# All scores of a pair of heads in one stretch: causal attention with three score buffers, ahead of a routed expert layer

## The chip, the cores and the metric

One core of one Trainium2 chip. The metric is the device time of one execution in microseconds (us), median of several; all values are fp32.

## The reference, cut to what matters

```python
# q, k, v: (8 batches, 8 heads, 576, 64), s: (8, 8, 576)
scores = q @ k.T / sqrt(64)                       # causal
cum = cumsum(maximum(s, 0), axis=-1)
bias = -(cum[:, :, :, None] - cum[:, :, None, :])
attn = exp(scores + minimum(bias, 0) - max)       # masked above the diagonal
attn = attn / (attn.sum(-1) + 1e-9)
x = (attn @ v) -> (8, 576, 512)
# then a router picks one of 8 experts per token (with a "locality gate" that can
# keep the previous token's expert): out = p[e] * (relu(x @ w1[e]) @ w2[e]), 512 -> 1024 -> 512
```

A pair of heads goes through these steps: score products and exponentials, products with the values, row sums (for the division), a product that turns the result back to rows of tokens and carries the router's weights along (the "turn back"), and the divisions. The kernel works through 32 pairs of heads in some 300 us and then through the experts in some 560 us. The routing of finished batches (sorting tokens by expert) is slipped in between pairs of heads, from about the tenth pair on.

## The kernel before

TensorE writes its products into banks of PSUM; the other engines read them there. Of the eight banks that the kernel uses, two score buffers take four, and four single banks hold values (`o0`, `o1`) and the turned-back result (`b0`, `b1`). The scores of a pair come in four units, two at a time, with work of the pairs before in between:

```python
def sums(n):                  # row sums: one-column products with a column of ones
    ...
                    for p in (p, P - TL) if 2 * g + t == NF else (p,):
                        mm(xs["o", 1][p : p + TL, i : i + 1], lhsT=w, rhs=one, start=True, stop=True)
    nc.vector.reciprocal(recs[:, n], xs["o", 1][:, at : at + 2 * NB])
# ... cut
for n in range(NPAIR + 1):
    # ... loads cut
    if n < NPAIR:
        scores(n, 0)                              # products, ScalarE exponentials, GpSimd masks
        scores(n, 1)
    if n:
        values(n - 1, 0, (0, 1))
        values(n - 1, 1, (0, 1))
        add_up(n - 1)                             # VectorE additions, for the sums
        copy(n - 1, 0)                            # VectorE: values out of PSUM
    if n > 1:
        back(n - 2, 1)                            # rows(): turn back; divide(): VectorE divisions
    for f in plan.pop((n, 0), ()): f(bank)        # routing work
    if n < NPAIR:
        scores(n, 2)
        scores(n, 3)
    if n:
        values(n - 1, 1, (2, 3, NF))
        sums(n - 1)                               # ends in bank o1, like group 1 of the values
        copy(n - 1, 1)                            # reads o1: after the sums
        back(n - 1, 0)                            # into b0
    for f in plan.pop((n, 1), ()): f(bank)
```

Of the kernel before, what the change touches and what calls it, by code (L numbers as in the profile page):

```python
# [10 lines left out]
F32 = mybir.dt.float32  # L11
I32 = mybir.dt.int32
Act = mybir.ActivationFunctionType
Alu = mybir.AluOpType
# [32 lines left out]
GROUPS = ((0, 2 * P), (2 * P, S))  # L47
MIDS = (P, 13 * TL // 2)
# [3 lines left out]
    ((1, 0, P, 2 * P), (0, 0, 0, 2 * P), (NF, 1, TS, S)),  # L52
    ((0, 1, 2 * P, S), (3, 1, 3 * P, S)),
    ((1, 1, 2 * P, S),),
    ((2, 1, 2 * P, S),),
# [11 lines left out]
def kernel(  # L67
# [30 lines left out]
    with ExitStack() as main:  # L98
# [40 lines left out]
        tail = attention(tc, q, k, vm, s, w_gate, w_local, ident, lg, recs, const, new_x, plan)  # L139
        tables = sort.tables()  # L140
        check = in_range(main.enter_context(tc.tile_pool(name="g_sb", bufs=1)), nc, recs, sort.total, sort.ones, out_of)
        hooks = [(0, tail), (2, last.stages[0]), (6, last.stages[1]), (11, last.stages[2]),
# [49 lines left out]
def attention(ctx, tc, q, k, vm, s, w_gate, w_local, ident, lg, recs, keep, new_x, plan):  # L192
# [11 lines left out]

# [5 lines left out]
    def pool(name, bufs, **kw):  # L210
        return ctx.enter_context(tc.tile_pool(name=name, bufs=bufs, **kw))
# [5 lines left out]
    ps_s = pool("ps_s", 2, space=PSUM)  # L217
    ps_o = pool("ps_o", 1, space=PSUM)

# [46 lines left out]
    idle = ps_o.tile([P, 512], F32, name="idle", tag="b0")  # L266

    def spin(n):
        for i in range(n):
            mm(idle[:, :P], lhsT=ident, rhs=ident, start=True, stop=True)  # L270
# [9 lines left out]
    for g, (q0, q1) in enumerate(GROUPS):  # L280
        rel = t_in.tile([BH, q1], F32, name=f"rel{g}")
        nc.vector.tensor_scalar(rel, cum[:, :q1], cum[:, MIDS[g] : MIDS[g] + 1], None, Alu.subtract)
        for c, a in enumerate(KEYS):
            if a + P <= q1:
                tr(bps[:, at : at + BH], rel[:, a : a + P], ident[:BH, :BH])
                bias_of[c, g] = at
                at += BH
# [3 lines left out]
    nc.vector.memset(bias[: P - TL, at : at + BH], MASKED)  # L291
    tmp.close()
# [3 lines left out]
    def scores(n, u):  # L296

        b, hp = divmod(n, HP)
        qb, kb = ins[b]
        ps = ps_s.tile([P, 2, 512], F32, name="ps", tag="s")  # L300
        sc = scs[n, u] = p_sc.tile([P, 2, sum(z - a for _, _, a, z in UNITS[u])], F32, name=f"sc{u}")
        for c, g, a, z in UNITS[u]:
            at = PIECE[c, g][1]
            for h in range(2):
                d = slice(DH * h, DH * h + DH)
                mm(ps[:, h, at : at + z - a], lhsT=kb[d, hp, KEYS[c] : KEYS[c] + P], rhs=qb[d, hp, a:z],  # L306
                   start=True, stop=True)
        for c, g, a, z in UNITS[u]:
            at = PIECE[c, g][1]
            for h in range(2):  # L310
                i = bias_of[c, g] + 2 * n + h
                nc.scalar.activation(sc[:, h, at : at + z - a], ps[:, h, at : at + z - a], Act.Exp,  # L312
                                     bias=bias[:, i : i + 1], scale=scale)
        diag = [PIECE[c, g][1] for c, g, a, z in UNITS[u] if a == KEYS[c]]
        if diag:
            step = diag[1] - diag[0] if len(diag) > 1 else P
            x = sc[:, :, diag[0] : diag[0] + step * len(diag)].rearrange("p h (n c) -> p h n c", c=step)[:, :, :, :P]
            nc.gpsimd.affine_select(out=x, in_=x, compare_op=Alu.is_ge, fill=0.0, base=0,  # L318
                                    pattern=[[0, 2], [0, len(diag)], [1, P]], channel_multiplier=-1)
        if (NF, 1) in PIECE and PIECE[NF, 1][0] == u:  # L320
            at = PIECE[NF, 1][1]
            x = sc[:, :, at : at + TL]
            nc.gpsimd.affine_select(out=x, in_=x, compare_op=Alu.is_ge, fill=0.0, base=P - TL,
                                    pattern=[[0, 2], [1, TL]], channel_multiplier=-1)

    def piece(n, c, g, a=0):

        u, at, q0, q1 = PIECE[c, g]
        at += max(0, a - q0)
        return scs[n, u][:, :, at : at + q1 - max(a, q0)]  # L330

    def add_up(n):

        add = nc.vector.tensor_tensor
        low = xs["sum", 0] = p_sm.tile([P, 2, P], F32, name="sum0")
        add(low, piece(n, 0, 0, P), piece(n, 1, 0), op=Alu.add)
        high = xs["sum", 1] = p_sm.tile([P, 2, S - 2 * P], F32, name="sum1")
        add(high, piece(n, 0, 1), piece(n, 1, 1), op=Alu.add)
        for c in (2, 3, NF):
            x = high[:, :, PIECE[c, 1][2] - 2 * P :]  # L340
            add(x, x, piece(n, c, 1), op=Alu.add)  # L341

    def values(n, g, cs):

        b, hp = divmod(n, HP)
        q0, q1 = GROUPS[g]
        if cs[0] == 0:
            xs["o", g] = ps_o.tile([P, 512], F32, name=f"o{g}", tag=f"o{g}")
        o = xs["o", g]
        for c in cs:  # L350
            a, z = PIECE[c, g][2:]
            w = piece(n, c, g)
            for h in range(2):
                mm(o[DH * h : DH * h + DH, a - q0 : z - q0], lhsT=vas[b % 2][:, c, 2 * hp + h, :], rhs=w[:, h],  # L354
                   start=(c == 0), stop=(c == (1, NF)[g]))

    def copy(n, g):
        q0, q1 = GROUPS[g]
        x = xs["t", g] = (keep if g else p_sm).tile([P, q1 - q0], F32, name=f"xT{g}")
        nc.vector.tensor_copy(x, xs["o", g][:, : q1 - q0])  # L360

    def halves(g):

        q0, q1 = GROUPS[g]
        for a in range(0, q1 - q0, TL):
            yield a // P, a, a % P

    def sums(n):

        at = S - 2 * P  # L370
        for g in range(2):
            for h in range(2):
                for t, a, p in halves(g):
                    w = piece(n, 0, 0) if g + t == 0 else xs["sum", g]
                    w = w[:, h, (a if g + t == 0 or g else a - P) :][:, :TL]
                    i = at + 2 * (2 * g + t) + h
                    for p in (p, P - TL) if 2 * g + t == NF else (p,):
                        mm(xs["o", 1][p : p + TL, i : i + 1], lhsT=w, rhs=one, start=True, stop=True)  # L378
        nc.vector.reciprocal(recs[:, n], xs["o", 1][:, at : at + 2 * NB])

    def rows(n, g, ps):
        hp = n % HP
        w = turn[:, hp].rearrange("p h w -> p (h w)")
        for t, a, p in halves(g):
            mm(ps[p : p + TL, t * 2 * HW : (t + 1) * 2 * HW], lhsT=xs["t", g][:, a : a + TL], rhs=w,  # L385
               start=True, stop=True)

    def divide(n, g, ps):

        b, hp = divmod(n, HP)  # L390
        if (b, "x") not in xs:
            xs[b, "x"] = new_x(b)
        for t0, t1, m in (((0, 2, P),), ((2, 4, P), (4, 5, TL)))[g]:
            k, i = t1 - t0, t0 - 2 * g
            x = xs[b, "x"][:m, t0:t1, 2 * hp * HW : (2 * hp + 2) * HW].rearrange("p t (h w) -> p t h w", w=HW)
            y = ps[:m, 2 * i * HW : 2 * (i + k) * HW].rearrange("p (t h w) -> p t h w", h=2, w=HW)
            rec = recs[:m, n, 2 * t0 : 2 * t1].rearrange("p (t h) -> p t h", h=2)
            nc.vector.tensor_tensor(x, y, rec.unsqueeze(3).to_broadcast([m, k, 2, HW]), op=Alu.mult)

# [13 lines left out]
    def back(n, g, ps=None):  # L413
        ps = ps_o.tile([P, 512], F32, name=f"b{g}", tag=f"b{g}") if ps is None else ps
        rows(n, g, ps)
        divide(n, g, ps)
        if g and n % HP == HP - 1:
            logits(n // HP)

    for n in range(NPAIR + 1):  # L420
        b, hp = divmod(n, HP)
        if b + 1 < B:
            if hp == 0:
                new_batch(b + 1)
            load_qk(b + 1, slice(hp, hp + 1))
            if hp == 1:
                load_v(b + 1, slice(0, HP))
        if n < NPAIR:
            scores(n, 0)
            scores(n, 1)  # L430
        if n:
            values(n - 1, 0, (0, 1))
            values(n - 1, 1, (0, 1))
            add_up(n - 1)
            copy(n - 1, 0)
        else:
            spin(8)
        if n > 1:
            back(n - 2, 1)
        for f in plan.pop((n, 0), ()):  # L440
            f(bank)
        if n < NPAIR:
            scores(n, 2)
            scores(n, 3)
        if n:
            values(n - 1, 1, (2, 3, NF))
            sums(n - 1)
            copy(n - 1, 1)
            back(n - 1, 0)
        else:  # L450
            spin(8)
        for f in plan.pop((n, 1), ()):
            f(bank)
    assert not plan
    return lambda bank: back(NPAIR - 1, 1, bank(1)[0])
# [786 lines left out]
```

## Time and profile before

| | before |
|---|---|
| median of 3 runs | 866.54 us (865.88 to 870.08) |
| profiled run | span 865.4 us, mean granted TensorE clock 0.997 |
| period of one pair of heads, no routing work beside it | 8.63 us |
| first expert product starts at | 302.06 us |

The prediction below shows and reads the lines of the page of the profiled run and of its chain: the work that ended last, followed back step by step to what each piece waited for. The granted clock is the share of full speed that TensorE was allowed. "Period" is the time from one pair's first scores to the next pair's.

### The profile page before, as it was taken

The numbers are of one execution on the slowest core, as the hardware profiler recorded it, in microseconds if no ns is written. First come the engines' busy times: TensorE is split into PE (matmuls) and PEld (weight loads), VectorE is DVE, ScalarE is ACT, GpSimd is POOL, SyncE is SP. The second block draws the span as 40 slices with busy tenths as digits, with TensorE's granted clock in tenths as the row PEclk, the third lists the DMA queues.
The fourth block names the chain that finished last, engine by engine and source line by source line (L and its number), as shares of the span: only waits on it lengthen the run. The fifth ranks groups of instructions, "written<-read, shape, count | busy, mean of one in ns | idle before, by whom it ended". The sixth has DMA issues, their size and how long they took to land.

```text
span 865.4 us, 17612 instructions
## 1 busy us (share of the span) xinstructions
PE 847.9 (98%) x7051; PEld 594.0 (69%) x7051; DVE 314.1 (36%) x837; ACT 185.5 (21%) x493; POOL 188.5 (22%) x289
## 2 busy tenths in 40 slices
PE   9999999999999999999899999999999999999996
PEld 7777677776777786586577766677657755776662
DVE  3566776678787757301111111111111111111111
ACT  5565555545555300000000000000000000000000
POOL 4322327226454205201110011000111001100001
PEclk9999999999999999999999999999999999999999
DMA  9163155833542609996599766994689935996001
GB/s 312 38 200 122 51 172 179 313 119 143 181 148 84 230 6 300 409 394 206 206 340 394 279 204 222 348 394 175 235 300 373 380 132 202 320 400 254 21 13 39
DMA packets 61403, 191.24 MB, mean 221 GB/s; under 512 B 7965, under 2 KB 9277, under 8 KB 61312
## 3 DMA queue, kind: packets, MB, share of 16 engines
q1 hardware_dynamic: 52272, 159.27, 51.9%
q0 software_dynamic: 8896, 30.47, 9.4%
q8 instruction: 57, 0.93, 0.4%
q10 hardware_dynamic: 144, 0.29, 0.1%
q14 instruction: 34, 0.28, 0.1%
HBM read 166.76 MB, written 23.76 MB: 220 GB/s over the span
## 4 chain that ended last, share of the span: by engine, by line
PE 97%; DVE 1%; issue 1%; POOL 0%; POOLq 0%; DVEq 0%
PE yp L1150 30%; PE hp L1126 28%; PE ps L306 11%; PE o L354 11%; PE b L385 5%; PE o L378 4%; PE hp L1133 4%; PE xp L1101 2%; PE idle L270 1%; DVE r_u L925 0%; DVE r_v L926 0%; PE bank L921 0%; PE bank L936 0%; PE bank L954 0%; PE bank L955 0%
## 5 line engine op out<-in xcount | busy, mean ns | idle before, releaser
L1150 PE MATMUL yp<-w,hT 128*128 128x512 f32 (+1 forms) x528 | 221.1, 594 | 0.0
L1126 PE MATMUL hp<-xT,w 128*128 128x256 f32 (+1 forms) x1088 | 193.8, 339 | 1.9 <-DVE xT L1104 1.9
L1126 PEld LDWEIGHTS hp<-xT,w 128*128 128x128 f32 x1088 | 173.2, 192 | 26.4 <-issue 7.8
L312 ACT ACTIVATE sc<-ps,bias 128x320 f32<-128x320 f32 (+4 forms) x448 | 160.4, 466 | 117.2 <-issue 56.5
L1150 PEld LDWEIGHTS yp<-w,hT 128*128 128x128 f32 (+1 forms) x528 | 88.0, 180 | 100.5 <-issue 99.5
L1157 POOL DMA_INDIRECT out_dram<-y,at x38 | 38.4, 1012 | 457.6 <-DVE y L1156 442.7
L1141 ACT ACTIVATE hT<-hp 128x512 f32<-128x512 f32 x38 | 22.7, 597 | 509.5 <-PE hp L1126 425.6
L306 PE MATMUL ps<-qk 64*128 64x320 f32 (+4 forms) x896 | 109.0, 377 | 3.1 <-DVE r_v L926 2.8
L1139 DVE TENSOR_SCALAR hT<-hp 128x512 f32<-128x512 f32 x38 | 26.2, 690 | 220.4 <-PE hp L1126 187.7
L354 PE MATMUL o<-sc,va 128*64 128x320 f32 (+4 forms) x896 | 100.8, 364 | 0.0
L318 POOL TENSOR_SCALAR_AFFINE_SELECT sc<-sc 128x256 f32<-128x256 f32 (+1 forms) x96 | 59.2, 616 | 149.2 <-ACT sc L312 101.4
L306 PEld LDWEIGHTS ps<-qk 64*128 64x128 f32 x896 | 71.6, 186 | 25.6 <-issue 5.9
L354 PEld LDWEIGHTS o<-sc,va 128*64 128x64 f32 x896 | 56.8, 136 | 42.3 <-issue 18.6
L1156 DVE TENSOR_SCALAR y<-yp,gate 128x512 f32<-128x512 f32 x38 | 28.5, 751 | 134.8 <-PE yp L1150 134.8
L341 DVE TENSOR_TENSOR sum<-sum,sc 128x640 f32<-128x640 f32 (+2 forms) x96 | 61.6, 642 | 9.8 <-POOL sc L318 4.9
L1150 PE MATMUL yp<-x,hT 128*128 128x512 f32 (+1 forms) x144 | 64.8, 595 | 0.0
L1104 DVE COPY xT<-xp 128x512 f32<-128x512 f32 x38 | 26.2, 690 | 81.2 <-PE xp L1101 81.0
L385 PE MATMUL b<-turn,xT 128*64 128x146 f32 x566 | 50.5, 291 | 0.0
L1126 PE MATMUL hp<-xT,x 128*128 128x128 f32 (+1 forms) x320 | 50.1, 317 | 0.0
L1126 PEld LDWEIGHTS hp<-xT,x 128*128 128x128 f32 x320 | 46.1, 191 | 5.8 <-issue 2.6
L990 POOL DMA_INDIRECT x_rows<-x,r_slot_i x40 | 43.3, 1083 | 11.4 <-issue 8.5
L385 PEld LDWEIGHTS b<-turn,xT 128*64 128x64 f32 x566 | 38.6, 137 | 7.8
(156 smaller groups left out, 552.9 us busy)
## 6 DMA issues: line engine op xcount, KB each, us to landing
w<-in_w_dram SPq DMA_DIRECT2D x184, 512.0 KB, 8.4
x<-in_w_dram SPq DMA_DIRECT2D x56, 512.0 KB, 9.6
qk<-in_q_dram SPq DMA_DIRECT2D x32, 288.0 KB, 4.8
va<-in_vm_dram SPq DMA_DIRECT2D x35, 256.0 KB, 4.1
qk<-in_k_dram SPq DMA_DIRECT2D x31, 288.0 KB, 5.1
xg<-x_rows POOLq DMA_DIRECT2D x30, 293.0 KB, 8.6
x_rows<-r_empty SPq DMA_DIRECT2D x6, 293.0 KB, 4.2
xg<-x_rows SPq DMA_DIRECT2D x4, 293.0 KB, 5.2
```

What stands on the lines that cost most here:

```text
L306: mm(ps[:, h, at : at + z - a], lhsT=kb[d, hp, KEYS[c] : KEYS[c] + P], rhs=qb[d, hp, a:z], start=True, stop=True)
L312: nc.scalar.activation(sc[:, h, at : at + z - a], ps[:, h, at : at + z - a], Act.Exp, bias=bias[:, i : i + 1], scale=scale)
L318: nc.gpsimd.affine_select(out=x, in_=x, compare_op=Alu.is_ge, fill=0.0, base=0, pattern=[[0, 2], [0, len(diag)], [1, P]], channel_multipli ...
L341: add(x, x, piece(n, c, 1), op=Alu.add)
L354: mm(o[DH * h : DH * h + DH, a - q0 : z - q0], lhsT=vas[b % 2][:, c, 2 * hp + h, :], rhs=w[:, h], start=(c == 0), stop=(c == (1, NF)[g]))
L378: mm(xs["o", 1][p : p + TL, i : i + 1], lhsT=w, rhs=one, start=True, stop=True)
L385: mm(ps[p : p + TL, t * 2 * HW : (t + 1) * 2 * HW], lhsT=xs["t", g][:, a : a + TL], rhs=w, start=True, stop=True)
L990: self.s.nc.gpsimd.indirect_dma_start(out=next(self.s.views)[:, :], out_offset=bass.IndirectOffsetOnAxis(ap=self.slot[:z, m : m + 1], axis=0),
L1126: mm(y, lhsT=w[0][:, c, f : f + P], rhs=xT[i][:, c, :], start=(c == 0), stop=(c == DK - 1))
L1133: mm(y[d, m], lhsT=w[h ^ swap][:, c, f + h * HALF : f + h * HALF + HALF], rhs=xT[i][:, c, m], start=(c == 0), stop=(c == DK - 1))
L1150: mm(ps[n * m : n * m + m, :], lhsT=hT[i][:, c, a : a + m], rhs=wn[:, c, :], start=(c == 0), stop=(c == FK - 1))
L1157: nc.gpsimd.indirect_dma_start(out=next(outs)[:, :], out_offset=bass.IndirectOffsetOnAxis(ap=at[i, k][:, 0:1], axis=0), in_=y[:, :], eleme ...
```

## The change

The intent is to change TensorE's shape of product less often: all scores of a pair in one stretch, all other products of the pair before it in the next, so one passage each way per pair instead of two. Three double score buffers take six of the eight banks. The other two serve everything else, shared by column: values (0 to 320 and 0 to 256), turned-back tiles (0 to 438 and 0 to 292), sums (438 to 448 of bank 1) and a small 64-column score unit (448 to 512 of both). Queries are grouped as 320 and 256 instead of 256 and 320. The core of the diff:

```diff
+    banks = [ps_o.tile([P, 512], F32, name=f"o{g}", tag=f"o{g}") for g in range(2)]
+    SUMS, LAST = 3 * 2 * HW, 512 - TL
# ... cut: units, bias columns, masks, additions regrouped
@@ def values(n, g)
+        ...  products into banks[g] ...
+        x = xs["t", g] = p_sm.tile([P, q1 - q0], F32, name=f"xT{g}")
+        nc.vector.tensor_copy(x, banks[g][:, : q1 - q0])
@@ def sums(n)
-                        mm(xs["o", 1][p : p + TL, i : i + 1], lhsT=w, rhs=one, start=True, stop=True)
+                        mm(banks[1][p : p + TL, i : i + 1], lhsT=w, rhs=one, start=True, stop=True)
@@ rows() and divide() become one
+    def back(n):
+        for t0, t1, m in ((0, 3, P), (3, NF, P), (NF, NB, TL)):
+            k, ps = t1 - t0, banks[t0 >= 3]
+            ...
+            for t in range(t0, t1):
+                for a, g, at, p in halves(t):
+                    mm(ps[p : p + TL, t - t0], lhsT=xs["t", g][:, at : at + TL], rhs=w, start=True, stop=True)
+            ...
+            nc.vector.tensor_tensor(x, y, rec.unsqueeze(3).to_broadcast([m, k, 2, HW]), op=Alu.mult)
@@ the loop over pairs
+        if n:
+            add_up(n - 1)
         if n < NPAIR:
-            scores(n, 0)
-            scores(n, 1)
# ... cut: the rest of the old order
+            for u in range(len(UNITS)):
+                scores(n, u)
         for f in plan.pop((n, 0), ()):
             f(bank)
         if n:
-            values(n - 1, 1, (2, 3, NF))
+            values(n - 1, 0)
+            values(n - 1, 1)
             sums(n - 1)
-            copy(n - 1, 1)
-            back(n - 1, 0)
+            back(n - 1)
# ... cut
-    return lambda bank: back(NPAIR - 1, 1, bank(1)[0])
```

## The prediction

No term of its sum is among them: -11.0 + 22.4 + 22.3 - 4 - 0.5 came to +29 us on 866.5, so 896 us, and stands whole. The lost 0.09 to 0.10 us and the exposed loads are read from the passages at 125.81 and 126.94 shown: the record of the first pass of the new shape is 533 ns for the 429 of the later ones into scores, and 483 for 432 out of them. The fence with L938 and L939 stands as the test of whether waits go by bank, which waits A and B then assume. That an fp32 product is two passes is read from the counts: 384 passes of 320 columns at L306, for 32 pairs, two heads and three pieces.

> **What bounds the kernel now.** I read the page first (busy shares, slices, the chain that ended last), then the chain in order of time over one pair of heads, then TensorE's timeline in very narrow windows, then the groups by form.
>
> ```profile
> PE 847.9 (98%) x7051; PEld 594.0 (69%) x7051; DVE 314.1 (36%) x837; ACT 185.5 (21%) x493; POOL 188.5 (22%) x289
> ...
> PEclk9999999999999999999999999999999999999999
> ...
> PE yp L1150 30%; PE hp L1126 28%; PE ps L306 11%; PE o L354 11%; PE b L385 5%; PE o L378 4%; PE hp L1133 4%; PE xp L1101 2%; PE idle L270 1%; DVE r_u L925 0%; DVE r_v L926 0%; PE bank L921 0%; PE bank L936 0%; PE bank L954 0%; PE bank L955 0%
> ```
>
> TensorE is busy 98% of the span, so time moves only by (a) how long its own stream takes and (b) new holes in it. The change touches attention alone: the first 300 us, 32 pairs. One pair in the chain, in order of time (start, length, what):
>
> ```profile
> 123.48 1.88 PE o L354 x16
> 125.36 0.74 PE b L385 x10
> 126.10 1.28 PE ps L306 x8
> 127.38 1.13 PE o L354 x12
> 128.50 1.12 PE o L378 x39
> 129.62 0.55 PE b L385 x8
> 130.17 1.94 PE ps L306 x20
> ```
>
> The period is 8.63 us (123.48 to 132.11), all TensorE: scores (L306) twice, in between values (L354), sums (L378) and the turn back (L385). Four times per pair the stream passes between scores (64 rows by 128 columns) and the others (128 rows by 64 columns). Waits in this stage are small: the list of waits has one line over a microsecond for TensorE's scores.
>
> ```profile
> PE ps L306 <- DVE r_v L926: 2.8, 4, 0.7
> ```
>
> What a passage costs, from narrow windows of TensorE's timeline (start, length, instructions; an fp32 product is two passes, and both heads' passes start together):
>
> ```profile
> 125.81 0.29 PE L385 MATMUL b<-turn,xT 128*64 128x146 f32 x1
> 126.03 0.54 PE L306 MATMUL ps<-qk 64*128 64x320 f32 x2
> 126.40 0.70 PE L306 MATMUL ps<-qk 64*128 64x320 f32 x4
> 126.67 0.70 PE L306 MATMUL ps<-qk 64*128 64x320 f32 x4
> 126.94 0.44 PE L306 MATMUL ps<-qk 64*128 64x320 f32 x2
> 127.31 0.49 PE L354 MATMUL o<-sc,va 128*64 128x320 f32 x2
> 127.62 0.60 PE L354 MATMUL o<-sc,va 128*64 128x320 f32 x4
> ```
>
> Within a stretch a 320-column pass follows every 0.27 us (126.40, 126.67, 126.94). Out of scores: 126.94 to 127.31 is 0.37, so 0.09 lost, and the first pass takes 0.32 to the next (0.05 lost): 0.146 us with the unrounded starts. Into scores: a 146-column pass streams 0.12 us, but 125.81 to 126.03 is 0.22 (0.096 lost), and 126.03 to 126.40 is 0.37 (0.107 lost): 0.203. A round trip costs **0.35 us**.
>
> [...]the first load after a passage into scores is exposed by 0.107, out of them, at 64 columns, by 0.053. [...]
>
> ```profile
> 120.90 1.09 PE L306 MATMUL ps<-qk 64*128 64x128 f32 x12
> 122.09 0.37 ACT L312 ACTIVATE sc<-ps,bias 128x128 f32<-128x128 f32 x1 [3.17 <-issue]
> 111.30 0.44 PE L936 MATMUL bank<-ident,r_v 2*128 2x2 f32 x5
> 111.80 0.15 DVE L938 COPY r_etok<-bank 128x8 f32<-128x8 f32 x1
> 111.87 0.14 DVE L939 COPY r_etok<-bank 64x2 f32<-64x2 f32 x1
> ```
>
> The 12 passes are a whole unit of three pieces. The first exponential reads only the first piece, done by 121.39, yet an idle ScalarE starts 0.10 us after the unit's last pass (121.99); the lag is the same 97 ns at three other pairs that I looked at. L938 reads only the first four blocks of a bank and starts after the fifth, and L939, which reads the fifth, carries no wait of its own.
>
> **The change part by part.**
>
> *Removed: one round trip per pair.* All scores are now one stretch: 0.35 x 31.5 = **-11.0 us**. Score columns stay 1600 per head in 7 products; values stay at 1600 columns with 8 pieces for 7 (a few ns of issue). The 64-column unit comes first now; its short passes expose the same two loads as they did inside unit 0. ScalarE gets 16 exponentials for 14: from the means by form (539, 479, 469, 362, 336 ns with overlap) some 5.5 grows to 6.05 us per pair, inside a period over 8: free.
>
> *Added, wait A: the sums behind the copy.* The copy of group 1 (L360) now stands before the sums, which write the same bank. By bank, TensorE must wait. From the start of the last values pass (64 columns, 0.222 long): 0.222 + 0.047 (the usual lag from TensorE's end to VectorE's start, at L379 and L398) + 0.415 (copy of 256) + 0.057 (lag back to TensorE, at L962 to L306) = 0.741, plus 0.053 for an exposed load. Without the wait the second pass of the sums would start at 0.082. A = 0.794 - 0.082 = 0.71, say **0.70 us x 32 = 22.4**.
>
> *Added, wait B: the next scores behind the divisions.* The first unit of the next pair (64 columns) goes to the last columns of the two banks that the divisions (L398) still read. Durations:
>
> ```profile
> L360 DVE COPY xT<-o 128x256 f32<-128x256 f32 x31 | 12.8, 414 | 0.0
> L398 DVE TENSOR_TENSOR x<-b,recs 128x292 f32<-128x292 f32 x63 | 28.9, 458 | 7.6 <-PE b L385 7.5
> L398 DVE TENSOR_TENSOR x<-b,recs 64x146 f32<-64x146 f32 x31 | 9.0, 292 | 0.0
> ```
>
> They grow by (458-292)/146 = 1.14 ns per element, so the new one of 438 elements takes 0.62, the two of 146 take 0.29 each, and neighbours overlap by 0.08 (read where two stand together). Let the turn back start at 0: its sixth pass starts at 0.646 and ends at 0.934; the large division runs 0.98 to 1.605, the next to 1.81, the last to 2.02; TensorE goes on at 2.08. Without the wait scores would start at 1.138 + 0.122 + 0.096 = 1.356. B = **0.72 us x 31 = 22.3**. [...]the exposed load is as before.
>
> *The routing work between pairs.* Its products (some 0.54, 0.37 and 0.62 us for each of four groups, L921, L936 and L954/L955) stand mostly after the turn back and so fall into hole B: -6. The old waits on them (L306 behind L926 and L962, 3.2 us) go, as there are three score buffers: -3.2. But their VectorE work (2.9 us at L925 to L928, about 2 at two others) now comes ahead of the additions (3.6 us) and the copies. A copy of group 1 is wanted 6.05 us after scores start, additions and first copy take 4.03, so 2.0 us are free and about 1.3 us per group overflow: +5. Sum **-4**.
>
> *Ends.* Eight warm-up products fewer, the last turn back inside attention: -0.5.
>
> Sum: -11.0 + 22.4 + 22.3 - 4 - 0.5 = +29 on 866.5, **896 us**. The expert stage is TensorE-bound (454.5 busy of 460 us from 400 to 860), so nothing there absorbs it.
>
> **The rivals.** *Waits by columns, not banks.* The columns used are carefully disjoint, as if that sufficed. Then A and B vanish and 866.5 - 11 - 3.2 - 1 gives 851, within 2%. Against it: the 97 ns lag and L939. I give it 4%. *VectorE becomes the bound.* It is busy 195 of 276 us between 24 and 300, and additions and divisions are now serial with TensorE's holes; if additions slow down (L338 took 1.25 us once against a mean of 0.88) the copies come late at many pairs: 905 to 915. For: its share; against: the 2 us of slack. *The compiler's order or an early load hides part of a hole* (weights loaded before the wait, divisions short): A and B at 0.5 each give 881. *The clock drops in the holes*: [...]before it stayed at 9 tenths or more through holes of 0.7. Unlikely.
>
> **Range and chances.** A and B are each good to about 0.12 us, 8 us in sum; routing to 4; the rivals stretch both ends: 882 to 909. Slower by over 2% (above 883.9): 0.86; within 2%: 0.11; faster: 0.03.
>
> **What would show it.** In the profile after: one passage each way per pair; a period near 9.7 us; a wait of TensorE's sums on the copy of group 1, 32 times about 0.6 to 0.7; a wait of the scores on the division, 31 times about 0.7 to 0.8; TensorE's busy time down by some 11 us while the span grows. No wait at the sums or first scores would make bank-wide waiting wrong; waits on the additions (L341) would speak for VectorE.

## The result, and the profile after

Median 963.62 us (four runs, 957.41 to 968.62) against 866.90 us for the kernel before beside it: ratio 1.1105, interval 1.1032 to 1.1178. Slower by 11%: direction as predicted, size not (+97 us for +29, above the range). All outputs are right. Here and below a ratio is the mean time of one kernel's fast runs over that of the other's fast runs of the same rounds, so not quite the ratio of the medians quoted.

The page of the changed kernel: busy times, granted clock by slice of 24 us, chain by line.

```profile
PE 893.0 (93%) x7164; PEld 645.2 (67%) x7164; DVE 322.4 (34%) x870; ACT 197.8 (21%) x557; POOL 184.3 (19%) x321
...
PEclk9999987798997777999999999999999999999999
...
PE yp L1132 28%; PE hp L1108 25%; PE ps L316 10%; PE o L357 8%; PE o L392 5%; PE o L378 5%; PE hp L1115 3%; DVE x L396 3%; PE o L316 2%; PE xp L1083 2%; DVE xT L360 2%; DVE sum L346 1%; DVE sum L343 1%; DVE r_v L910 1%; DMA s_sb<-in_s_dram 0%
```

Two things are new. VectorE is now in the chain that ends last: divisions (L396), copies (L360) and even additions (L343, L346). And the clock, which never left 9 tenths before, sits at 7 or 8 in eight slices between 120 and 385 us. Lines are now L316 for scores, L357 for values, L378 for sums, L392 for the turn back.

One pair in the chain in order of time (start, length, what), without routing work:

```profile
100.20 2.89 PE o L357 x32
...
103.19 0.44 DVE xT L360
...
103.67 1.33 PE o L378 x40
105.00 0.82 PE o L392 x12
...
105.84 0.84 DVE x L396 x2
...
106.73 0.46 PE o L392 x2
107.19 0.36 PE o L316 x2
...
107.59 0.32 PE o L316
```

TensorE stops three times, where the prediction has two. **Hole A**: the sums (103.67) wait for the copy of group 1. **Hole C**, not predicted: the turn back has run 16 of its 18 passes (the chain shows the 12 that release the first division) and waits for two divisions (105.84 to 106.68) before its last two, which write the bank that the second division reads. **Hole B**: the second product of the next pair's small unit (107.59) waits for the last division. The period is 10.46 us for 8.63. The list of waits (total us, times, longest) counts A and C:

```profile
PE o L378 <- DVE xT L360: 24.8, 32, 2.5
PE o L392 <- DVE x L396: 20.7, 31, 0.7
```

The predicted wait of the scores on the division, 31 times 0.7 to 0.8, is not in the list. Its place is the turn back's, 20.7 / 31 = 0.67 us each.

TensorE by stretches (us; busy and instructions of PE, PEld, DVE, ACT, POOL; granted clock; DMA share; GB/s):

```profile
16.00:121.00 105.00, 91.92 (x1191) 72.11 (x1187) 58.79 (x142) 54.76 (x164) 26.78 (x64) 1.00 0.32 106
121.00:190.00 69.00, 61.79 (x627) 48.13 (x625) 34.04 (x89) 29.92 (x89) 22.22 (x41) 0.78 0.37 126
190.00:380.00 190.00, 165.41 (x1880) 129.43 (x1876) 107.57 (x298) 82.32 (x246) 58.40 (x109) 0.86 0.35 120
```

For 105 us, ten pairs, the holes are there and the clock is full. Then it drops, to 0.78 on average. The records show it at half speed in spells of 3.4, 6.8 and 10.2 us, 92.6 us in all (before: 7.9 us). These sums run to the end of the record; each run's last 3.6 to 6.7 us of half clock come after its last product. PE's busy time rises by 45 us although the work is the same, because a product at half clock takes double the time (256-column passes of the scores follow each other in 0.43 us after 132 us, in 0.22 us after 98 us), and a record's end reaches into the hole behind it (the last pass of the values before the hole of 103.67 starts at 102.85 and its record is 0.22 us long, though such a pass of 64 columns is followed by the next after 0.056 us); so "busy" was no measure of what was saved.

One more place differs, the handover to the experts. First before, then changed; the first line of each is what follows the last scores, the last line the first expert product:

```profile
290.20 1.13 PE o L354 x12
...
298.69 0.90 PE bank L385 x10
...
302.06 4.06 PE hp L1126 x11
```

```profile
373.96 2.89 PE o L357 x32
...
380.94 4.43 PE o L357 x26
...
392.95 5.45 PE hp L1108 x24
```

Cut by these marks, the two profiled runs (865.4 and 955.8 us) compare so:

| stretch | before | changed | difference |
|---|---|---|---|
| first scores to the second pair's | 7.3 | 5.1 | -2.2 |
| 30 periods, second pair's scores to the last pair's | 268.7 | 354.2 | +85.5 |
| last pair's scores to the first expert product | 17.8 | 25.3 | +7.5 |
| first expert product to the end | 563.3 | 562.9 | -0.4 |

So nothing is lost in the experts. Of the +85.5, 30 x (10.46 - 8.63) = 54.9 is the undisturbed period. The rest is the pairs beside routing work or at half clock: they add 354.2 - 30 x 10.46 = 40.4 us to undisturbed pairs, where before they added 268.7 - 30 x 8.63 = 9.8.

### The profile page after: what moved, and what is told of

Its sections match the earlier page's. It is cut to its first block, busy times and chain, and to the rows that moved or that the text cites. A ratio compares the mean times of both kernels' runs of the same rounds, so it can differ in the third digit from the quotient of the medians.

```text
span 955.8 us, 18004 instructions
## 1 busy us (share of the span) xinstructions
PE 893.0 (93%) x7164; PEld 645.2 (67%) x7164; DVE 322.4 (34%) x870; ACT 197.8 (21%) x557; POOL 184.3 (19%) x321
## 4 chain that ended last, share of the span: by engine, by line
PE 88%; DVE 8%; issue 2%; DMA 1%; ACT 0%; POOL 0%; DVEq 0%; SPq 0%; POOLq 0%; ACTq 0%
PE yp L1132 28%; PE hp L1108 25%; PE ps L316 10%; PE o L357 8%; PE o L392 5%; PE o L378 5%; PE hp L1115 3%; DVE x L396 3%; PE o L316 2%; PE xp L1083 2%; DVE xT L360 2%; DVE sum L346 1%; DVE sum L343 1%; DVE r_v L910 1%; DMA s_sb<-in_s_dram 0%
## 5 line engine op out<-in xcount | busy, mean ns | idle before, releaser
L322 ACT ACTIVATE sc<-ps,bias 128x256 f32<-128x256 f32 (+3 forms) x448 | 155.1, 480 | 29.1 <-PE ps L316 25.5
L316 PE MATMUL ps<-qk 64*128 64x192 f32 (+2 forms) x768 | 122.4, 465 | 0.0
L316 PEld LDWEIGHTS ps<-qk 64*128 64x128 f32 x768 | 99.3, 237 | 14.4 <-issue 3.7
L357 PE MATMUL o<-sc,va 128*64 128x256 f32 (+3 forms) x1024 | 96.1, 340 | 0.0
L357 PEld LDWEIGHTS o<-sc,va 128*64 128x64 f32 x1024 | 67.2, 139 | 32.0 <-issue 5.8
L329 POOL TENSOR_SCALAR_AFFINE_SELECT sc<-sc 128x256 f32<-128x256 f32 x128 | 61.3, 482 | 120.0 <-ACT sc L322 107.1
L392 PE MATMUL o<-turn,xT 128*64 128x146 f32 x576 | 58.0, 309 | 21.4 <-DVE x L396 20.7
L346 DVE TENSOR_TENSOR sum<-sum,sc 128x128 f32<-128x128 f32 (+2 forms) x128 | 62.4, 487 | 4.4
L392 PEld LDWEIGHTS o<-turn,xT 128*64 128x64 f32 x576 | 39.1, 144 | 30.5 <-DVE x L396 30.5
L360 DVE COPY xT<-o 128x320 f32<-128x320 f32 x64 | 28.7, 456 | 69.1 <-PE o L357 68.9
L396 DVE TENSOR_TENSOR x<-o,recs 128x438 f32<-128x438 f32 (+2 forms) x96 | 36.2, 405 | 40.8 <-PE o L392 40.8
```

The lines of the kernel that those rows point to most:

```text
L316: mm(ps[h][:, at : at + z - a], lhsT=kb[d, hp, KEYS[c] : KEYS[c] + P], rhs=qb[d, hp, a:z], start=True, stop=True)
L322: nc.scalar.activation(sc[:, h, at : at + z - a], ps[h][:, at : at + z - a], Act.Exp, bias=bias[:, i : i + 1], scale=scale)
L329: nc.gpsimd.affine_select(out=x, in_=x, compare_op=Alu.is_ge, fill=0.0, base=0, pattern=[[0, 2], [1, P]], channel_multiplier=-1)
L346: add(y, y, piece(n, c, g), op=Alu.add)
L357: mm(banks[g][DH * h : DH * h + DH, a - q0 : z - q0], lhsT=vas[b % 2][:, c, 2 * hp + h, :], rhs=w[:, h], start=(c == 0), stop=(c == cs[-1]))
L360: nc.vector.tensor_copy(x, banks[g][:, : q1 - q0])
```

## The experiments

**Theory**: bank-wide waits make three holes (A, B, C), and together they leave TensorE too little work in some windows, so that its clock halves. **Rivals**: (1) the holes are not those waits, or VectorE is the bound; (2) the clock has another cause, and the lower clock is only beside the holes.

| kernel | undisturbed period | half clock, whole record | median us | ratio to before, interval |
|---|---|---|---|---|
| before | 8.63 | 7.9 | 866.9 | 1 |
| changed | 10.46 | 92.6 | 963.62 | 1.1105, 1.1032 to 1.1178 |
| e1, without C | 9.81 | 88.6 | 934.78 | 1.0737, 1.0696 to 1.0778 |
| e2, without A | 9.65 | 59.0 | 925.31 | 1.0675, 1.0617 to 1.0732 |
| e3, without B | 10.00 | 143.5 | 989.62 | 1.1331, 1.1284 to 1.1378 |
| e4, without all three | 8.28 | 40.4 | 886.44 | 1.0209, 1.0170 to 1.0248 |
| e5, holes filled | 10.46 | 29.9 | 934.36 | 1.0735, 1.0676 to 1.0793 |
| e7, e4 with routing spread | 8.28 | 15.8 | 867.99 | 0.9905, 0.9866 to 0.9945 |
| e8, e7 in two stretches | 8.63 | 7.6 | 869.29 | 0.9941, 0.9904 to 0.9977 |
| e9, e7 spread later | 8.28 | 20.1 | 862.36 | 0.9897, 0.9845 to 0.9949 |
| e10, e3 with holes filled | 10.00 | 24.1 | 926.81 | 1.0670, 1.0612 to 1.0728 |
| e11, before + A alone | 9.44 | 44.7 | 917.12 | 1.0544, 1.0494 to 1.0595 |
| e12, wide sums | 10.46 | 26.9 | 932.80 | 1.0740, 1.0698 to 1.0783 |
| e13, e3 with wide sums | 10.00 | 26.5 | 924.01 | 1.0630, 1.0596 to 1.0664 |

Four calls, each with its own runs of the kernel before: e1, e2, e4, e5; e3, e7, e8 (before there 874.99, on another chip); e9, e10, e11; e12, e13. Edits are against the changed kernel unless said.

### One hole at a time: e1, e2, e3

e1 makes all turn-back products before the divisions, so that no product follows a division of its bank:

```diff
+        turned = []
         for t0, t1, m in ((0, 3, P), (3, NF, P), (NF, NB, TL)):
             ... products ...
+            turned.append((t0, t1, m, k, ps))
+        for t0, t1, m, k, ps in turned:
             ... division ...
```

> The changed kernel with one edit: the turn back's last products (tile 4, bank 1) stand before the divisions. My prediction had no wait there; the trace of the changed kernel shows one, 31 times about 0.68 us idle (0.855 us from product to product beyond the usual distance), because the division of tile 3 reads the bank that tile 4's products write. If that omission is the wrong step: the wait at L392 behind L396 is gone, the wait of the next scores grows from some 0.45 to some 0.72 us, the undisturbed period falls from 10.46 to about 9.9 us, and the time to 903 us plus whatever the clock still loses (0 to 33 us): 905 to 940. Rival, that the excess is the lower clock alone and the hole costs nothing: period and time stay at 10.46 and 957 to 968.

Met. The period falls by 0.65 us.

e2 makes the values of group 1 first, so that its copy runs beside the products of group 0:

```diff
-            values(n - 1, 0)
             values(n - 1, 1)
+            values(n - 1, 0)
             sums(n - 1)
```

> The changed kernel with the two groups of values swapped (group 1 and its copy first), so that the copy of bank 1 is done long before the sums write that bank. If waiting goes by banks: the wait of the sums behind the copy (0.77 us per pair) vanishes, no new one at the turn back (the copy of bank 0 hides under 1.33 us of sums), period about 9.7 us, time about 897 plus the clock's loss: 900 to 935. If waits go by something else (tile or program order), the sums wait for the later copy just as long: period 10.46, time 957 to 968.

Met. In an undisturbed pair the sums follow the values without a wait, and the period falls by 0.81 us. In these banks a bank and a buffer of the program are the same, so e2 cannot tell waits by bank from waits by buffer. One place in the kernel before can: a routing buffer of two banks, where VectorE starts to read the first bank (L925, 101.87 us) while TensorE's product into the second still runs (L921, to 101.97), and the same at 173.89, 211.03 and 247.98 us.

e3 puts the small unit, which shares the divisions' banks, second in the score stretch, with its exponentials still first:

```diff
-            for u in range(len(UNITS)):
-                scores(n, u)
+            for us in ((1, 0), (2,), (3,)):
+                for u in us:
+                    products(n, u)
+                for u in us[::-1]:
+                    exps(n, u)
```

> The changed kernel with only the 64-column unit moved to second place in the score stretch (its exponentials still first). Takes away the wait of the next scores behind the last division and nothing else. In the changed kernel I read 0.45 us per pair for it from the distance of products. Theory: period 10.0 us, the waits of the sums (L378 behind L360) and of the last turn products stay; time 957 to 968 minus 14, so 935 to 955, clock still below 0.97. Rival: the hole is only handed on, as the divisions end at the same time and the unit still needs them: period 10.46.

A clear miss. The period falls by 0.46 us as it should, 14 us in all, yet the kernel is longer than the changed one. The granted clock shows where:

```profile
PEclk9898977788777787899999999999999999999999
```

143.5 us of half clock, and already in the pairs without routing work. All four runs had a lower clock (0.919 to 0.928) than any of the changed kernel (0.941 to 0.953). Here taking out a hole cost time: a ratio of 1.1331 for 1.1105.

### All three, and what is left: e4

e4 is e1, e2 and e3 together.

> All three holes removed: products before divisions, group 1 first, and the 64-column unit in second place of the score stretch, with its exponentials issued first. One passage each way per pair stays. Theory (three bank waits, and the clock falls only because of them): period 8.63 - 0.35 = 8.3 us, clock 1.00, time 866.9 - 11 - 3 = about 853 us (848 to 860), faster than the kernel before by 1 to 2 per cent. Rival (the stretches themselves are slower, or VectorE with its 3.6 us of additions becomes the bound): 867 or more, with waits behind L346.

The period is right: 8.28 us, which is the 8.63 before less the 0.35 that one round trip was predicted to cost. So rival (1) falls for the undisturbed pair: the three bank-wide waits are its whole loss, 10.46 - 8.28 = 2.18 us. The total is a miss, and the chain through a pair with routing work says why:

```profile
113.01 1.11 PE o L385 x39
...
119.27 0.48 DVE sum L350
...
123.84 0.43 DVE xT L367
...
124.31 1.78 PE o L385 x33
```

Between two runs of the sums (L385) everything in the chain but one short turn back is VectorE: divisions, routing operations to 119.27, additions (L350), more routing, then the copy (L367) that the sums need. VectorE as the bound holds for these pairs alone, and all five spells of half clock during attention fall in pairs longer than 8.28 us.

### Is it the clock? e5, e10, e12, e13

e5 leaves every wait and puts unread products of 384, 448 and 192 columns into the three holes:

```diff
+    def fill(n, cols):
+        v = vas[n // HP % 2][:, 0].rearrange("p h d -> p (h d)")
+        for h in range(2):
+            mm(xs["fill"][DH * h : DH * h + DH, :cols], lhsT=v[:, :DH], rhs=v[:, :cols], start=True, stop=True)
```

> The changed kernel with all its waits, but the three holes are filled with products that nobody reads (384, 448 and 192 columns, both column halves, into a score buffer). They end before the wait does. Theory that TensorE's clock falls because the holes and the one-column sums leave it idle: no interval at half clock, granted clock 0.99 or more, period still 10.46 us in each pair, time about 957 - 33 = 925 us (918 to 932). Rival, that the clock falls for another reason or that the lower clock costs nothing on the path: clock 0.95 and 957 to 968 as before.

The time is just above what was expected, and the half clock has not quite gone: 29.9 us are left, at a clock of 0.985 in the profiled run. The period stays 10.46, and with more work on TensorE the kernel is some 32 us shorter (by the ratios, 0.037 of 867).

To see what lowers the clock I went through the records of nine traces. Clock changes fall on a grid of 3.41 us (every spell at either clock in the changed kernel's record, but the one after its last product, is a multiple of 3.413 us: 3.413, 6.827, 10.240 and so on to 570.026). For each window of that grid I added up the time in which columns stream through TensorE, at 0.833 ns per column of a pass (in the kernel before, passes of values follow each other in 269 ns at 320 columns and in 56 ns at 64, so 213 ns for 256 columns). A one-column product of the sums then counts almost nothing, though two of them, side by side, keep their place for 58 ns until the next two start (the text of e12 has 52 ns). In every trace the windows with a share above some 39% kept the clock and those below it were followed by half clock. On this rest two runs that take no wait away. e12 gives the sums 48 columns of ones for one; the other 47 results are overwritten or unread:

```diff
+WIDE = 48
-    one = keep.tile([P, 1], F32, name="one")
+    one = keep.tile([P, WIDE], F32, name="one")
-                        mm(banks[1][p : p + TL, i : i + 1], lhsT=w, rhs=one, start=True, stop=True)
+                        mm(banks[1][p : p + TL, i : i + WIDE], lhsT=w, rhs=one, start=True, stop=True)
```

> The changed kernel with its waits, order and instructions untouched; only the sums' moving operand is 48 columns of ones instead of 1, so that each of the 40 passes streams 40 ns instead of 1 inside its 52 ns slot (the surplus columns are overwritten or lie free; the result stays right). Worked out from nine traces: the clock fell after just those 3.41 us windows in which products streamed for under some 39 per cent of the time, never after others. Theory that this share decides: each pair gains some 0.8 us of streaming just where it is short, so most windows at 0.30 to 0.39 rise above 0.5, half clock falls from 85 us to under 25, the undisturbed period stays 10.46, and the time falls to 925 to 940, ratio 1.065 to 1.08. Rival (holes in TensorE's queue, not streaming, decide): clock and ratio as in the changed kernel, 0.95 and 1.11.

Met but for the half clock, 26.9 us for under 25: the same instructions, waits and period, some 31 us less. The stretches of e12 that answer to the last two above:

```profile
121.00:190.00 69.00, 58.51 (x755) 45.97 (x753) 42.05 (x105) 35.74 (x108) 26.61 (x46) 1.00 0.52 178
190.00:380.00 190.00, 158.59 (x1925) 125.96 (x1922) 116.26 (x327) 77.22 (x233) 55.93 (x104) 0.96 0.32 114
```

0.78 has become 1.00, 0.86 has become 0.96. Rival (2) falls: it is the little streaming in and around the holes that lowers the clock.

e13 is e3 with the same wide sums, e10 is e3 with unread products in holes A and C.

> The same edit on e3 (the 64-column unit second), which had the most half clock, 144 us, and ratio 1.133. Theory: half clock under 40 us, undisturbed period 10.0, ratio 1.06 to 1.085, thus now faster than the changed kernel, as its shorter period had promised. Rival: ratio near 1.13.

> The kernel with the 64-column unit second (e3: undisturbed period 10.0 us, yet 990 us and 144 us at half clock), with its two remaining holes filled with unread products of 384 and 448 columns. Theory that e3 was slow by its clock alone: period stays 10.0, under 30 us at half clock, and about 0.45 us saved per microsecond of half clock taken away: 990 - 50 = 940 or less, ratio 1.06 to 1.08. Rival (something else in e3 is slow, say ScalarE's order): ratio 1.11 or more with a clock above 0.98.

Both met. The 0.45 us per microsecond of half clock in e10's text was the author's estimate; e10's profiled run has 119.4 us less half clock than e3's and 60.2 us less time, 0.50. e13's clock:

```profile
PEclk9999999999999899999999999999999999999999
```

117 us less half clock than e3, and 60.1 us less span (982.6 to 922.5). Now e3's edit pays: its shorter period promises 30 x 0.46 = 13.8 us, and e13 is 8.8 us below e12 (the other 5 I did not trace). So it was the clock that made e3 longer than the changed kernel.

Over all 14 traces, 1377 windows between 15 and 390 us were at full clock from end to end. The 89 followed by half clock had a share of 0.390 or less; the other 1288 had 0.390 or more. So sharp a line needs one fitted number: each window is taken to end some 0.11 us before the recorded change. Without this lag the two groups overlap between 0.36 and 0.42, and about a dozen windows lie on the wrong side. With the same lag the line holds where it was not drawn, from 390 us to each trace's last product: of 2086 windows at full clock, the 14 followed by half clock had 0.391 or less, the others 0.400 or more. An undisturbed pair of the changed kernel has a share down to 0.30, and 12% of the places where a window can lie are under 0.39; in the kernel before the lowest is 0.57, in e12 0.56. Whether a window meets such a place depends on where the pairs happen to lie on the grid. Once it did, pairs grew to 12.7 to 13.8 us (the four from 130 to 183 us), near four windows (13.65), so the next pair lay the same way: the falls at 128.0, 141.6, 155.3, 169.0 and 182.6 us are 13.65 apart, as four windows are. That e3 met them more often than the changed kernel, with the same 12%, I put down to this placing; I did not test it, and as all four runs of e3 show it, the chance start of one run does not explain it.

### The one wait alone, in the kernel before: e11

Against the kernel before; its four banks and its order stay, only the copy of group 1 now stands ahead of the sums that share its bank:

```diff
             values(n - 1, 1, (2, 3, NF))
-            sums(n - 1)
             copy(n - 1, 1)
+            sums(n - 1)
             back(n - 1, 0)
```

> The kernel before with one edit: the copy of group 1 moved ahead of the sums, as the changed kernel has it. The columns differ, only the bank is the same. If waiting goes by banks, TensorE waits for the copy at the start of each pair's sums: 0.70 (my prediction's A for 256 columns) plus 0.01 for 320 columns, up to 0.77 as seen in the changed kernel, so 32 x 0.71 to 0.77 = 23 to 25 us: ratio 1.025 to 1.03, period 9.35 us. If by columns: ratio 1.00. If the clock drops with one hole of this size alone: more than 1.035.

```profile
101.96 0.50 DVE xT L360
...
102.51 1.33 PE o L378 x40
```

Hole A appears by itself: 8.63 to 9.44, 0.81 us, as e2 took away. That is 26 us, about as expected for waits by bank (23 to 25); the other 21 of the 47 come with 37 us more half clock, the case of the expectation's last sentence. One hole of 0.8 us per pair is enough: the sums, 1.33 us of one-column products, follow it, and the least share of an undisturbed pair is 0.37.

### Can the idea pay? e7, e8, e9

e7 is e4 with the routing operations of VectorE dealt out over a pair, a few after each group of products, instead of in one block:

```diff
+PULL = (0.6, 0.6, 0.8, 0.5)                      # about so many us of VectorE work at each place
+            pull(PULL[0])
             values(n - 1, 1)
+            pull(PULL[1])
+            values(n - 1, 0)
+            pull(PULL[2])
             sums(n - 1)
+            pull(PULL[3])
             back(n - 1)
+            pull(99)
```

> The kernel without the three holes, whose undisturbed period was 8.28 us but which took 886 us, with the routing work's VectorE operations dealt out over a pair (some before the copy of group 1, some between the copies, after them, after the reciprocal and after the divisions) in place of standing in one block ahead of the additions. Theory: what was left over there, eleven waits of the sums behind a late copy (up to 2.4 us) and six spells at half clock, comes from that block; so the disturbed periods fall from 8.9 to 14 us to under 9.2, the clock stays at 0.99 or more, and the time is 866.9 - 11 - 3 plus a few = 850 to 858, faster than the kernel before. Rival (VectorE has too little time whatever the order, or the clock falls in the sums themselves): 875 or more, clock below 0.985.

Partly met. By the ratios 26 us of e4's time are gone (1.0209 to 0.9905). The median lies 10 us above the range, with the kernel before 8 us slower on this chip too. Pairs with routing take 9.1 to 9.6 us and some over 10, the routing's first product waiting for ScalarE to free a score buffer.

e8 is e7 with the last score unit moved between the two groups of values, which brings the second round trip back (its "tiling modes" are the two shapes of product, 64*128 and 128*64 in the traces):

> The same with one more round trip between the two tiling modes per pair: the last score unit is issued between the two groups of values. Theory: 0.35 us per pair more, 11 us over 32 pairs, so e7's time plus 9 to 13. Rival (the passages cost nothing that is not hidden): the same time as e7 within 2 us.

The period is 0.35 us longer, as expected. The total is not, only 1.3 us (3 by the ratios), as its rival said: e8's pairs with routing take about as long as e7's (9.0 to 9.9 us for 9.1 to 9.6), and no spell of half clock falls in its attention. e9 is e7 with `PULL = (0, 0.6, 0.8, 0.5)`:

> The spread kernel (e7) with one number changed: the routing work of a pair starts after the copy of group 1, not before the values. In e7 its first product waited up to 1.2 us for ScalarE, because it takes the score buffer whose exponentials are not done by then, in each of some twelve pairs. Theory: those waits vanish, disturbed periods fall from 9.3 to 9.7 us to below 9, undisturbed ones stay 8.28, clock 0.99 or more: e7's ratio to the kernel before, 0.9905, falls to 0.975 to 0.985. Rival (the routing work only shifts its delay to the divisions): ratio 0.99 or more.

It missed the expected ratio by 0.005; pairs with routing take 9.0 to 9.2 us. Its ratio is the lowest, about 1% under the kernel before and so within the 2%, and the intervals do not tell it from e7's. Its first expert product starts at 291.15 us instead of 302.06, but from there it takes 569.4 us for 563.3. While products run there, it has 8.5 us more half clock (12.0 for 3.4 us), which at half speed can be 4.3 us, and TensorE stops for 2.2 us more (6.12 for 3.95, counting stops of over 0.3 us). The clock fell there by the same rule: the windows that hold e9's stops at 402 and 714 us have shares of 0.07 and 0.391 and were followed by half clock, those with the stops of the kernel before at 412 and 720 us have 0.401 and 0.407 and were not. Why these stops differ stays open.

## Why the prediction was wrong, point by point

**Right**: the passages cost 0.35 us a round trip (e4, e9 at 8.28; e8 back at 8.63). Waits go by bank (period 10.46 to 9.65 us in e2, 8.63 to 9.44 in e11; L925 in the kernel before starts 0.1 us before the record of the product into the buffer's other bank ends). Experts absorb nothing and gain nothing (-0.4 us). Hole A was sized at 0.70 and measured 0.81. Hole B was sized at 0.72, and that is what it is once C is gone: e1's 9.81 less A (0.81) less 8.28 is 0.72. (One sum among the rivals is off: A and B at 0.5 give 882.5, not 881.)

**Wrong, term by term**, on the profiled runs (+90.4 us):

| term of the prediction's sum | predicted | measured | where |
|---|---|---|---|
| round trip, A and B | -11.0 + 22.4 + 22.3 = +33.7 | +54.9 | 30 x (10.46 - 8.63) |
| the clock | 0 ("unlikely") | +25.6 | spans of changed less e12 |
| routing work between pairs | -4 | +5 | 40.4 - 25.6 - 9.8 |
| ends | -0.5 | +5.3 | +7.5 - 2.2 of the table |
| sum | +29 | +90.8 | less 0.4 in the experts |

- The step that failed first is **wait B**: "Let the turn back start at 0: its sixth pass starts at 0.646 ...; TensorE goes on at 2.08". It lets all of the turn back run ahead of the divisions. The diff does not: the division stands inside the loop over tiles, so tile 4's products follow tile 3's division in the same bank. The wait by bank had been read from the trace (the 97 ns lag and L939) and used twice; its third place was missed. Together A, B and C cost 2.18 us per pair instead of 1.42.
- The largest single term is **the clock**: "before it stayed at 9 tenths or more through holes of 0.7" took a hole's length for what counts. What stood before each of the 89 falls counted during attention was little streaming in a 3.41 us window, a share of 0.390 or less. The term is more than the 25.6 us of the profiled runs in the medians: e12 is 31 us below the changed kernel, whose other three runs had clocks of 0.941 to 0.946 against the profiled 0.953.
- **Routing**: with the clock cured (e12) pairs beside it still add 14.8 us to undisturbed ones, three spells of half clock among them, against 9.8 before. The 6 us that its products were to save in hole B do not show in this sum; I did not take it apart. Its VectorE work delays copies: the sums waited up to 2.5 us, in the changed kernel and, at full clock, in e12.
- **Ends**: with all other products of a pair behind all its scores, two pairs' worth, with their holes, follows the last scores. First expert products came 19.0 us after them instead of 11.9.

Of these, the holes and the clock are shown by runs that take each away; the ends are read from two traces and not tried separately.

## What to carry to other kernels

List for every bank its writers and readers in program order and count a wait wherever the engine changes (here one cost 0.81 us per pair for A, 0.65 for C and 0.46 to 0.72 for B); do it again for each loop in which products and their readers alternate, not only where two blocks meet. A stop that recurred with every pair cost twice here, once for its length and once beside a lower TensorE clock (26 and 21 us in e11), so work out how much of each 3.4 us TensorE streams columns: here under 39% meant half clock, and wider products in the place of the tiny ones took away most of it (26.9 us left of 92.6) without removing a stop. And when VectorE stands between two products of TensorE, any other work in its queue at that place stands there too (the sums waited up to 2.5 us here).
